# Attention backward on one core: three buffers for dV and dK, four for K^T and V^T, transposing DMAs placed tick by tick

## The chip, the cores and the metric

The kernel runs on one core of a Trainium2 chip. The metric is the device time of one execution in microseconds (us), lower is better; ten runs of the kernel before are at hand, and one of them was profiled.

## The reference

Two attention blocks, A and B, share the shapes: 8 batches, 96 query tokens, model width 640, 32 heads of 128, a cache of 512 keys. The outputs are the forward result and all gradients, so the keys and values are read and their gradients written for every head and batch.

```python
def block(x, k_cache, v_cache, wq, wo):       # x (8, 96, 640), caches (8, 32, 512, 128)
    q = (x @ wq).reshape(B, Sq, H, Dh).transpose(0, 2, 1, 3)
    scores = einsum("bhqd,bhkd->bhqk", q, k_cache) * (Dh ** -0.5)
    p = softmax(scores, axis=-1)
    o = einsum("bhqk,bhkd->bhqd", p, v_cache)
    return o.transpose(0, 2, 1, 3).reshape(B, Sq, H * Dh) @ wo

out, vjp = jax.vjp(f, A_x, A_k_cache, A_v_cache, A_wq, A_wo, B_x, ...)   # f joins A and B on the last axis
return (out, *vjp(grad_out))                  # out, dx, dk_cache, dv_cache, dwq, dwo of A and of B
```

All arrays are bf16.

## The kernel before, in words

The unit of work is one head of one batch. Two heads of one batch make a pair (HP = 2) and share their transfers: a pair needs K and V in natural layout (tiles K_sb and V_sb, L257), K^T and V^T by transposing DMA (KT_p and VT_p, L246), and it stores dV and dK (tiles dV_sb and dK_sb, L266). Each of these six transfers moves 256 KB and is issued on the queue of SP, which issues in order. There are 256 pairs in the two blocks.

An Emitter collects all steps with a tick and a slot and emits them sorted. In each tick one unit starts, and other units are in later stages of the same pipeline (offsets in OFF): S = QK^T and its row maximum (s2: PE L286, DVE L288, ACT's exponent L298), 1/rowsum and P (s3: DVE L308, POOL L317), P transposed and dV = P^T dO (s4: PE L340 and L357, ACT copies L346 and L362), O^T (s5: PE L333, DVE L343, POOL's product with dO L371), dP and dS (s6: PE L381 and L383, DVE L385), dS transposed and dK (s7: PE L407 and L423, ACT copies to dK_sb at L428), dQ^T (s8: PE L400). In between, at slots of their own, stand the steps of a whole head (projections, their transposes and the weight gradients; slot HEAD) and those of a group of four heads (output sums, gU; slot GRP). The last group of a block writes its sums through tile ob (DVE L521) and a DMA on POOL's queue (L522).

Block B's x and grad_out are brought in and transposed while block A is still running: ten chunks of 192 KB go through the staging tile ld_tmp (pool stp, DMA on POOL's queue L113, PE transposes L131).

The framework gives each tile a number of buffers, inserts the waits and orders the instructions by priority: an instruction that reuses a buffer waits until the last reader of its earlier content is done. PSUM is one set of eight banks that all steps share. A store's buffer is free when the store has landed. Each engine runs its instructions in the order of the built program.

Before, the four transposing DMAs of two batches (two K^T, two V^T) are emitted together, one tick ahead of the first one's s2; KT_p has four buffers, VT_p six, dV_sb and dK_sb two, ob five, ld_tmp three.

Of the kernel before, what the change touches and what calls it, by code (L numbers as in the profile page):

```python
# [11 lines left out]
BF16 = mybir.dt.bfloat16  # L12
# [3 lines left out]
class Emitter:  # L16
    def __init__(self):
        self.items = []
        self.n = 0
# [21 lines left out]
SL_GRP = 95  # L41
SL_SETUP = 96

OFF = dict(t=-1, kn=3, vn=0, s2=3, s3=3, s4=4, s5=5, s6=6, s7=7, s8=8)
HP = 2
TB = 2
HK = [
    dict(pA=-10, pB=-7, pC0=[-6, -4], pC1=[-5, -3], pD1=-2, pD0=0, qA0=21, qA1=25, qB=[28, 25], qD=[(26, 0, 2), (27, 2, 5)]),
    dict(pA=-4, pB=-2, pC0=[-1, 3], pC1=[1, 2], pD1=3, pD0=6, qA0=29, qA1=33, qB=[36, 33], qD=[(34, 0, 2), (35, 2, 5)]),
# [3 lines left out]
PRIO_OFF = 2000  # L53
GSPREAD1 = 9
SLOTS = dict(LOAD=0, S2A=5, S2B=5.5, S8=10, S7=20, S5=30, S4=40, S6=50, S3A=52, S3B=53, S5B=54, HEAD=SL_HEAD, GRP=SL_GRP)


def build_block(tc, em, tick0, blk, x, kc, vc, wq, wo, g_all, out_all, dx, dk, dv, dwq, dwo, ident, ones, pools, HG=4, first=True, groups=None):
    nc = tc.nc
# [7 lines left out]
    KC = Sk // 128  # L67
# [10 lines left out]
    while t0 < T:  # L78
        w = 512 if T - t0 >= 512 else (256 if T - t0 >= 256 else (128 if T - t0 >= 128 else T - t0))
# [4 lines left out]
    while c0 < D:  # L84
        w = 512 if D - c0 >= 512 else (256 if D - c0 >= 256 else 128)
# [10 lines left out]
    const, ps, kvp, wk, hd, hst, grp = (pools[k] for k in ("const", "ps", "kvp", "wk", "hd", "hst", "grp"))  # L96
# [7 lines left out]
    CS = pools["CS"]  # L104

    stp = pools["stp"]

    def setup_ld(which_, c):
        def f():
# [129 lines left out]
    F4 = Sk // R8 // KC  # L239

    def p_ldT(h, b, which):
        def f():
            key = "KT" if which == 0 else "VT"
            t_ = kvp.tile([128, F4 * KC, 16], BF16, name=key + "_p", bufs=(4 if which == 0 else 6))
            src = (kc if which == 0 else vc)[b, h:h + HP].rearrange("h (r f) d -> (h r) (f d)", r=R8)
            nc.sync.dma_start_transpose(t_[:], src)  # L246
            for j in range(HP):
                half = t_[:, :, j * R8:(j + 1) * R8]
                CS.setdefault((blk, h + j, b), {})[key] = half.rearrange("p (f c) r -> p f c r", c=KC)
        return f  # L250

    def p_ldn(h, b, which):
        def f():
            key = "K_sb" if which == 0 else "V_sb"
            t_ = kvp.tile([128, HP, KC, 128], BF16, name=key, bufs=4)
            src = (kc if which == 0 else vc)[b, h:h + HP]
            nc.sync.dma_start(t_[:].rearrange("p h c d -> p h (c d)"), src.rearrange("h (p c) d -> p h (c d)", c=KC))  # L257
            for j in range(HP):
                CS[(blk, h + j, b)][key] = t_[:, j]
        return f  # L260

    def p_st(h, b, which):
        def f():
            t_ = CS[(blk, h, b)]["dV_p" if which == 1 else "dK_p"]
            dst = (dv if which == 1 else dk)[b, h:h + HP]
            nc.sync.dma_start(dst.rearrange("h (p c) d -> p h (c d)", c=KC), t_[:])  # L266
            if which == 0:
                for j in range(HP):
                    CS.pop((blk, h + j, b))
        return f  # L270
# [79 lines left out]
    def c_s4(h, b):  # L350
        def f():
            st = CS[(blk, h, b)]
            hs = HS[(blk, h)]
            P_sb = st["P_sb"]
            dV_ps = bank([128, KC * 128], F32, "dV_ps")
            for c in range(KC):
                nc.tensor.matmul(dV_ps[:, c * 128:(c + 1) * 128], P_sb[:, c * 128:(c + 1) * 128], hs["dOnat_h"][:, b * 128:(b + 1) * 128], start=True, stop=True)  # L357
            j = h % HP
            if j == 0:
                st["dV_p"] = wk.tile([128, HP, KC * 128], BF16, name="dV_sb", bufs=2)  # L360
            dV_p = CS[(blk, h - j, b)]["dV_p"]
            nc.scalar.activation(dV_p[:, j], dV_ps[:], ACT.Identity, scale=1.0)  # L362
        return f
# [52 lines left out]
    def c_s7(h, b):  # L416
        def f():
            st = CS[(blk, h, b)]
            hs = HS[(blk, h)]
            dS_sb = st["dS_sb"]  # L420
            dK_ps = bank([128, KC * 128], F32, "dK_ps")
            for c in range(KC):
                nc.tensor.matmul(dK_ps[:, c * 128:(c + 1) * 128], dS_sb[:, c * 128:(c + 1) * 128], hs["Qnat_h"][:, b * 128:(b + 1) * 128], start=True, stop=True)  # L423
            j = h % HP
            if j == 0:
                st["dK_p"] = wk.tile([128, HP, KC * 128], BF16, name="dK_sb", bufs=2)
            dK_p = CS[(blk, h - j, b)]["dK_p"]
            nc.scalar.activation(dK_p[:, j], dK_ps[:], ACT.Identity, scale=1.0)  # L428
        return f
# [70 lines left out]
    def gU(g, which, t, gi):  # L500
        def f():
            acc = S.get("out_acc" if which == 0 else "dx_acc")
            dst_flat = out_flat if which == 0 else dx_flat
            (c0, w) = gsplits[gi]
            o_ps = bank([128, w], F32, "o_ps")
            for hh in range(groups[g]):
                h = GH0[g] + hh
                src = HS[(blk, h)]["OT_h"] if which == 0 else HS[(blk, h)]["dQT_h"]
                rhs = G[g]["wo_r"][:, hh, c0:c0 + w] if which == 0 else HS[(blk, h)]["wqT_h"][:, c0:c0 + w]
                nc.tensor.matmul(o_ps[:], src[:, t * 128:(t + 1) * 128], rhs, start=(hh == 0), stop=(hh == groups[g] - 1))  # L510
            if NG == 1:
                ob = wk.tile([128, w], BF16, name="ob", bufs=5)
                evac(EV["gU"], ob[:], o_ps[:])
                nc.gpsimd.dma_start(dst_flat[t * 128:(t + 1) * 128, c0:c0 + w], ob[:])
            elif g == 0:
                evac(EV["gU"], acc[:, t, c0:c0 + w], o_ps[:])
            elif g < NG - 1:
                nc.vector.tensor_tensor(acc[:, t, c0:c0 + w], o_ps[:], acc[:, t, c0:c0 + w], op=ALU.add)
            else:
                ob = wk.tile([128, w], BF16, name="ob", bufs=5)  # L520
                nc.vector.tensor_tensor(ob[:], o_ps[:], acc[:, t, c0:c0 + w], op=ALU.add)  # L521
                nc.gpsimd.dma_start(dst_flat[t * 128:(t + 1) * 128, c0:c0 + w], ob[:])  # L522
        return f
# [4 lines left out]
    for g in range(NG):  # L528
        h0 = GH0[g]
        for hh in range(groups[g]):  # L530
            h = h0 + hh
# [4 lines left out]
            em.add(c0t + hk["pB"], SL_HEAD, pB(h))  # L536
            em.add(c0t + OFF["s5"], SL_LOAD, h_alloc(h))
            for si in range(NTS):
# [4 lines left out]
            for b in range(B):  # L543
                ct = c0t + b * HP + j
                if j == 0:
                    if b % TB == 0:
                        for which in (0, 1):
                            for bb in range(b, b + TB):
                                em.add(ct + OFF["t"], SLOTS["LOAD"] - 1, p_ldT(h, bb, which))
                    em.add(ct + OFF["kn"], SLOTS["LOAD"], p_ldn(h, b, 0))  # L550
                    em.add(ct + OFF["vn"], SLOTS["LOAD"], p_ldn(h, b, 1))
                    em.add(ct + HP + OFF["s4"], SLOTS["LOAD"], p_st(h, b, 1))
                    em.add(ct + HP + OFF["s7"] + 1, SLOTS["LOAD"], p_st(h, b, 0))
                em.add(ct + OFF["s2"], SLOTS["S2A"], c_s2a(h, b))
                em.add(ct + OFF["s2"], SLOTS["S2B"], c_s2b(h, b))
                em.add(ct + OFF["s3"], SLOTS["S3A"], c_s3a(h, b))
                em.add(ct + OFF["s3"], SLOTS["S3B"], c_s3b(h, b))
                em.add(ct + OFF["s5"], SLOTS["S5B"], c_s5b(h, b))
                em.add(ct + OFF["s4"], SLOTS["S4"], c_s4(h, b))
                S45.setdefault(ct + OFF["s5"], [None, None, None])[0] = (blk, h, b)  # L560
                S45.setdefault(ct + OFF["s4"], [None, None, None])[1] = (blk, h, b)
                S45.setdefault(ct + OFF["s6"], [None, None, None])[2] = (blk, h, b)
                S78.setdefault(ct + OFF["s8"], [None, None])[0] = (blk, h, b)
                S78.setdefault(ct + OFF["s7"], [None, None])[1] = (blk, h, b)
                em.add(ct + OFF["s6"], SLOTS["S6"], c_s6(h, b))
                em.add(ct + OFF["s7"], SLOTS["S7"], c_s7(h, b))
# [24 lines left out]
def _kernel_impl(tc, A_x, A_k_cache, A_v_cache, A_wq, A_wo, B_x, B_k_cache, B_v_cache, B_wq, B_wo, grad_out,  # L591
           out_0, out_1, out_2, out_3, out_4, out_5, out_6, out_7, out_8, out_9, out_10, HG=4, slots=None, off=None, hk=None, ev=None, gspread=None, groupsA=None, groupsB=None):
    global GSPREAD0, GSPREAD1
    nc = tc.nc
# [10 lines left out]
    with ExitStack() as ctx:  # L605
        P = lambda **kw: ctx.enter_context(tc.tile_pool(**kw))
# [5 lines left out]
        pools = dict(  # L612
            const=P(name="const", bufs=1),
            ps=P(name="ps", bufs=8, space=PSUM),
            kvp=P(name="kv", bufs=11),
            wk=P(name="wk", bufs=3),
            hd=P(name="hd", bufs=2),
            hst=P(name="hst", bufs=8),
            grp=P(name="grp", bufs=1),
            stp=P(name="stp", bufs=3),  # L620
        )
        pools["S45"] = {}
        pools["S78"] = {}
        pools["HS"] = {}
        pools["CS"] = {}
        em = Emitter()
# [78 lines left out]
```

## Time and profile before

| | |
|---|---|
| median of 10 runs | 1761.67 us (1754.67 to 1767.12) |
| the profiled execution | 1765.31 us |
| its span (first to last instruction) | 1763.5 us |
| mean granted TensorE clock | 0.986 |
| HBM | 161.09 MB read, 159.12 MB written |
| PE / DVE / ACT / POOL busy | 1644.3 / 1391.8 / 1349.8 / 710.3 us |
| median issue to landing, stores of dV and dK | 4.0 and 4.1 us |
| median issue to landing, transposing DMAs | 5.0 to 5.3 us |

The profile is one execution. PE is TensorE's matmuls, PEld its weight loads, DVE the vector engine, ACT the scalar engine, POOL GpSimd, SP the engine that only issues DMAs. A number behind an L is a line of the kernel. "A <- B" after a wait names what ended it. A matmul's end is modelled, and a few matmul records can be missing.

### The profile page before, as it was taken

How to read it: one execution, taken by the hardware profiler on the slowest of the kernel's cores; microseconds unless marked ns; L12 is line 12 of the kernel's file. 1: busy time of each engine (PE TensorE's matmuls, PEld its weight loads, DVE VectorE, ACT ScalarE, POOL GpSimd, SP SyncE). 2: the span in 40 equal slices, each digit the busy share in tenths (PEclk: the TensorE clock that was granted, in tenths of full speed). 3: DMA queues.
4: the chain of work that ended last, by engine and by line, in shares of the span. 5: the costliest groups of instructions: out<-in, count | busy, mean ns of one | idle time of the engine just before them, and what ended most of it. 6: DMA issues, size and time to landing. Idle time of an engine off the chain costs nothing. (4 is left out here: it accounts for less than half of the span.)

```text
span 1763.5 us, 59487 instructions
## 1 busy us (share of the span) xinstructions
PE 1644.3 (93%) x22474; PEld 1370.9 (78%) x22648; DVE 1391.8 (79%) x3597; ACT 1349.8 (77%) x3529; POOL 710.3 (40%) x1306
## 2 busy tenths in 40 slices
PE   6899989999999999998998999999999999999997
PEld 5687878788787888777776787787878778787776
DVE  4786778878888888877776778887888878888886
ACT  4888967878778787866776888787787877778782
POOL 3333434433433443334365334333433334333346
PEclk9999999999999999999999999999999999999999
DMA  9999999999999999999899999999999999999993
GB/s 262 264 273 270 264 251 259 273 260 274 268 267 277 254 283 261 255 268 257 217 284 282 261 269 264 265 266 271 262 264 260 254 270 258 260 271 248 262 256 114
DMA packets 320609, 458.39 MB, mean 260 GB/s; under 512 B 37216, under 2 KB 300896, under 8 KB 312128
## 3 DMA queue, kind: packets, MB, share of 16 engines
q1 hardware_dynamic: 304672, 404.75, 88.1%
q0 software_dynamic: 15648, 49.83, 8.4%
q8 instruction: 177, 2.90, 0.7%
q14 instruction: 112, 0.92, 0.2%
HBM read 161.09 MB, written 159.12 MB: 182 GB/s over the span
## 5 line engine op out<-in xcount | busy, mean ns | idle before, releaser
L298 ACT ACTIVATE E_sb<-S_ps,negm 96x512 bf16<-96x512 f32 x512 | 349.3, 682 | 211.6 <-DVE negm L288 200.5
L317 POOL TENSOR_SCALAR P_sb<-E_sb,rinv 96x512 bf16<-96x512 bf16 x512 | 352.4, 688 | 344.0 <-DVE rinv L308 339.2
L371 POOL TENSOR_TENSOR prod<-OT_h,dOT_h 128x96 bf16<-128x96 bf16 x512 | 187.1, 365 | 570.1 <-DVE OT_h L343 566.2
L385 DVE SCALAR_TENSOR_TENSOR dS_sb<-dP_ps,dl_ps,P_sb 96x512 bf16<-96x512 f32 x512 | 381.9, 746 | 35.0 <-PE dl_ps L383 22.0
L288 DVE TENSOR_REDUCE negm<-S_ps 96x1 f32<-96x512 f32 x512 | 347.5, 679 | 71.1 <-PE S_ps L286 70.4
L428 ACT ACTIVATE dK_sb<-dK_ps 128x512 bf16<-128x512 f32 x512 | 302.9, 592 | 116.4 <-PE dK_ps L423 69.5
L362 ACT ACTIVATE dV_sb<-dV_ps 128x512 bf16<-128x512 f32 x512 | 307.8, 601 | 20.0 <-DMA out_dram<-dV_sb 17.4
L346 ACT ACTIVATE PT_sb<-optp_ps 128x384 bf16<-128x384 bf16 x512 | 252.3, 493 | 0.5 <-PE optp_ps L340 0.5
L286 PE MATMUL S_ps<-KT_p,QT_h 128*96 128x512 bf16 x512 | 196.4, 384 | 23.4 <-ACT dK_sb L428 22.7
L423 PE MATMUL dK_ps<-Qnat_h,dS_sb 96*128 96x128 bf16 x2048 | 199.8, 220 | 6.0 <-ACT dV_sb L362 4.7
L357 PE MATMUL dV_ps<-dOnat_h,P_sb 96*128 96x128 bf16 x2048 | 200.4, 221 | 3.6 <-ACT dV_sb L362 3.6
L407 PE MATMUL dq_dst_ps<-ident,dS_sb 96*128 96x96 bf16 x2048 | 174.1, 207 | 26.9 <-DVE dS_sb L385 24.8
L381 PE MATMUL dP_ps<-VT_p,dOT_h 128*96 128x512 bf16 x512 | 197.4, 386 | 0.3 <-ACT dV_sb L362 0.3
L409 DVE COPY dST_sb<-dq_dst_ps 128x384 bf16<-128x384 bf16 x512 | 176.9, 345 | 15.8 <-PE dq_dst_ps L407 15.1
L340 PE MATMUL optp_ps<-ident,P_sb 96*128 96x96 bf16 x2048 | 173.4, 206 | 2.7 <-POOL P_sb L317 1.8
L333 PE MATMUL optp_ps<-PT_sb,V_sb 128*128 128x96 bf16 x2048 | 173.4, 207 | 2.1 <-ACT PT_sb L346 1.9
L400 PE MATMUL dq_dst_ps<-dST_sb,K_sb 128*128 128x96 bf16 x2048 | 172.5, 207 | 3.0 <-ACT dK_sb L428 2.2
L510 PE MATMUL o_ps<-wo_r,OT_h 128*128 128x256 bf16 (+1 forms) x1152 | 153.6, 258 | 1.5 <-ACT E_sb L298 0.5
L400 PEld LDWEIGHTS <-K_sb 128*128 128x128 bf16 x2048 | 135.5, 99 | 24.3 <-issue 4.9
L510 PE MATMUL o_ps<-wqT_h,dQT_h 128*128 128x256 bf16 (+1 forms) x1152 | 150.3, 255 | 0.0
L343 DVE CAST OT_h<-optp_ps 128x96 bf16<-128x96 f32 x512 | 126.3, 247 | 29.7 <-PE optp_ps L340 26.8
L308 DVE RECIPROCAL rinv<-rowsum 96x1 f32<-96x1 f32 x512 | 79.9, 156 | 86.4 <-ACT E_sb L298 64.7
(77 smaller groups left out, 3397.5 us busy)
## 6 DMA issues: line engine op xcount, KB each, us to landing
out_dram<-dV_sb SPq DMA_DIRECT2D x256, 256.0 KB, 4.0
out_dram<-dK_sb SPq DMA_DIRECT2D x256, 256.0 KB, 4.1
V_sb<-in_A_v_cache_dram SPq DMA_DIRECT2D x128, 256.0 KB, 4.0
K_sb<-in_A_k_cache_dram SPq DMA_DIRECT2D x128, 256.0 KB, 4.4
V_sb<-in_B_v_cache_dram SPq DMA_DIRECT2D x128, 256.0 KB, 4.1
K_sb<-in_B_k_cache_dram SPq DMA_DIRECT2D x128, 256.0 KB, 4.9
out_dram<-dwo_sb POOLq DMA_DIRECT2D x64, 160.0 KB, 4.9
out_dram<-dwq_sb POOLq DMA_DIRECT2D x32, 320.0 KB, 6.3
```

Source lines behind the costliest of these rows:

```text
L288: nc.vector.tensor_reduce(negm[:], S_ps[:], axis=AX.X, op=ALU.max, negate=True)
L298: nc.scalar.activation(E_sb[:].rearrange("q (a f) -> q a f", f=F4), st["S_ps"][:].rearrange("q (f a) -> q a f", f=F4), ACT.Exp, bias=st["n ...
L317: nc.gpsimd.tensor_scalar(P_sb[:], st["E_sb"][:], st["rinv"][:], 0.0, op0=ALU.mult, op1=ALU.add)
L346: nc.scalar.activation(PT_sb[:], PT_ps, ACT.Identity, scale=1.0)
L357: nc.tensor.matmul(dV_ps[:, c * 128:(c + 1) * 128], P_sb[:, c * 128:(c + 1) * 128], hs["dOnat_h"][:, b * 128:(b + 1) * 128], start=True, s ...
L362: nc.scalar.activation(dV_p[:, j], dV_ps[:], ACT.Identity, scale=1.0)
L381: nc.tensor.matmul(dP_ps[:], hs["dOT_h"][:, tok], st["VT"], start=True, stop=True)
L385: nc.vector.scalar_tensor_tensor(dS_sb[:].rearrange("q (a f) -> q a f", f=F4), dP_ps[:].rearrange("q (f a) -> q a f", f=F4), dl_ps[:, 0:1] ...
L400: nc.tensor.matmul(dQT_ps, st["K_sb"][:, c, :], st["dST_sb"][:, c * Sq:(c + 1) * Sq], start=(c == 0), stop=(c == KC - 1))
L423: nc.tensor.matmul(dK_ps[:, c * 128:(c + 1) * 128], dS_sb[:, c * 128:(c + 1) * 128], hs["Qnat_h"][:, b * 128:(b + 1) * 128], start=True, s ...
L428: nc.scalar.activation(dK_p[:, j], dK_ps[:], ACT.Identity, scale=1.0)
L510: nc.tensor.matmul(o_ps[:], src[:, t * 128:(t + 1) * 128], rhs, start=(hh == 0), stop=(hh == groups[g] - 1))
```

## The change

The transposing DMAs are no longer emitted in groups of four: K^T of a pair is emitted two ticks ahead of the pair's start and V^T one tick behind it, each among the other loads. VT_p goes from six buffers to four, dV_sb and dK_sb from two to three; ob goes from five to four and ld_tmp from three to two. The ticks of the other loads and stores are the same numbers written as offsets, with slots that put loads of K^T and V^T ahead of plain loads ahead of stores within a tick. The object Chain passes SP's DMAs through and keeps the last one; it orders nothing.

```diff
-OFF = dict(t=-1, kn=3, vn=0, s2=3, ...)
+OFF = dict(kt=-2, vt=1, vn=0, kn=3, dv=6, dk=10, s2=3, ...)
-TB = 2
+class Chain:
+    def __call__(self, res):
+        ins = getattr(res, "ins", res)
+        self.last = ins
+        return res
...
-            t_ = kvp.tile([128, F4 * KC, 16], BF16, name=key + "_p", bufs=(4 if which == 0 else 6))
+            t_ = kvp.tile([128, F4 * KC, 16], BF16, name=key + "_p", bufs=4)
...
-            nc.sync.dma_start_transpose(t_[:], src)
+            sp(nc.sync.dma_start_transpose(t_[:], src))
...
-                st["dV_p"] = wk.tile([128, HP, KC * 128], BF16, name="dV_sb", bufs=2)
+                st["dV_p"] = wk.tile([128, HP, KC * 128], BF16, name="dV_sb", bufs=3)
...
-                st["dK_p"] = wk.tile([128, HP, KC * 128], BF16, name="dK_sb", bufs=2)
+                st["dK_p"] = wk.tile([128, HP, KC * 128], BF16, name="dK_sb", bufs=3)
...
-                ob = wk.tile([128, w], BF16, name="ob", bufs=5)
+                ob = wk.tile([128, w], BF16, name="ob", bufs=4)
...
-                    if b % TB == 0:
-                        for which in (0, 1):
-                            for bb in range(b, b + TB):
-                                em.add(ct + OFF["t"], SLOTS["LOAD"] - 1, p_ldT(h, bb, which))
-                    em.add(ct + OFF["kn"], SLOTS["LOAD"], p_ldn(h, b, 0))
-                    em.add(ct + OFF["vn"], SLOTS["LOAD"], p_ldn(h, b, 1))
-                    em.add(ct + HP + OFF["s4"], SLOTS["LOAD"], p_st(h, b, 1))
-                    em.add(ct + HP + OFF["s7"] + 1, SLOTS["LOAD"], p_st(h, b, 0))
+                    em.add(ct + OFF["kt"], SLOTS["LOAD"], p_ldT(h, b, 0))
+                    em.add(ct + OFF["vt"], SLOTS["LOAD"], p_ldT(h, b, 1))
+                    em.add(ct + OFF["vn"], SLOTS["LOAD"] + 0.1, p_ldn(h, b, 1))
+                    em.add(ct + OFF["kn"], SLOTS["LOAD"] + 0.1, p_ldn(h, b, 0))
+                    em.add(ct + OFF["dv"], SLOTS["LOAD"] + 0.2, p_st(h, b, 1))
+                    em.add(ct + OFF["dk"], SLOTS["LOAD"] + 0.2, p_st(h, b, 0))
...
-            stp=P(name="stp", bufs=3),
+            stp=P(name="stp", bufs=2),
+        pools["sp"] = Chain(tc)
```

More of the change, by code (lines that the diff above doesn't have):

```diff
@@ L42 @@
 SL_SETUP = 96
-OFF = dict(t=-1, kn=3, vn=0, s2=3, s3=3, s4=4, s5=5, s6=6, s7=7, s8=8)
+OFF = dict(kt=-2, vt=1, vn=0, kn=3, dv=6, dk=10, s2=3, s3=3, s4=4, s5=5, s6=6, s7=7, s8=8)
 HP = 2
-TB = 2
 HK = [
@@ L55, with __init__ @@
 SLOTS = dict(LOAD=0, S2A=5, S2B=5.5, S8=10, S7=20, S5=30, S4=40, S6=50, S3A=52, S3B=53, S5B=54, HEAD=SL_HEAD, GRP=SL_GRP)
+class Chain:
+    def __init__(self, tc):
+        self.tc = tc
+        self.last = None
+    def __call__(self, res):
+        ins = getattr(res, "ins", res)
+        self.last = ins
+        return res
 def build_block(tc, em, tick0, blk, x, kc, vc, wq, wo, g_all, out_all, dx, dk, dv, dwq, dwo, ident, ones, pools, HG=4, first=True, groups=None):
@@ L106, in build_block @@
     stp = pools["stp"]
+    sp = pools["sp"]
     def setup_ld(which_, c):
@@ L256, in f @@
             src = (kc if which == 0 else vc)[b, h:h + HP]
-            nc.sync.dma_start(t_[:].rearrange("p h c d -> p h (c d)"), src.rearrange("h (p c) d -> p h (c d)", c=KC))
+            sp(nc.sync.dma_start(t_[:].rearrange("p h c d -> p h (c d)"), src.rearrange("h (p c) d -> p h (c d)", c=KC)))
             for j in range(HP):
@@ L265, in f @@
             dst = (dv if which == 1 else dk)[b, h:h + HP]
-            nc.sync.dma_start(dst.rearrange("h (p c) d -> p h (c d)", c=KC), t_[:])
+            sp(nc.sync.dma_start(dst.rearrange("h (p c) d -> p h (c d)", c=KC), t_[:]))
             if which == 0:
@@ L519, in f @@
             else:
-                ob = wk.tile([128, w], BF16, name="ob", bufs=5)
+                ob = wk.tile([128, w], BF16, name="ob", bufs=4)
                 nc.vector.tensor_tensor(ob[:], o_ps[:], acc[:, t, c0:c0 + w], op=ALU.add)
```

## The prediction

> **What bounds the kernel now.** I read the page first (busy shares, then the DMA queues), then the windows of the steady part, then the waits of ACT and PE in it, and last the timeline around single stalls. Columns of the windows: stretch, its length, busy time and instructions of PE, weight loads, DVE, ACT and POOL, granted clock, DMA share, GB/s.
>
> ```profile
> PE 1644.3 (93%) x22474; PEld 1370.9 (78%) x22648; DVE 1391.8 (79%) x3597; ACT 1349.8 (77%) x3529; POOL 710.3 (40%) x1306
> ...
> q1 hardware_dynamic: 304672, 404.75, 88.1%
> ```
> ```profile
> 60.00:1700.00 1640.00, 1551.01 (x21309) 1294.42 (x21474) 1315.03 (x3409) 1286.63 (x3374) 653.23 (x1199) 0.99 0.99 264
> ```
>
> Two resources look full: PE (1551 of 1640 us in the steady part, 89 us without a matmul) and the DMA engines (0.99). Which one sets the pace is decided by what the others wait for. The waits of that stretch (total us, times, longest):
>
> ```profile
> ACT dK_sb L428 <- DMA out_dram<-dK_sb: 34.4, 30, 2.7
> ACT dV_sb L362 <- DMA out_dram<-dV_sb: 17.4, 16, 2.4
> ```
> ```profile
> PE S_ps L286 <- ACT dK_sb L428: 22.1, 14, 2.7
> PE dq_dst_ps L407 <- DVE dS_sb L385: 19.8, 17, 1.6
> PE dl_ps L383 <- POOL prod L371: 5.9, 1, 5.9
> PE tp_ps L131 <- DMA ld_tmp<-in_B_x_dram: 5.7, 3, 3.5
> PE dK_ps L423 <- ACT dV_sb L362: 4.7, 4, 1.6
> PE dV_ps L357 <- ACT dV_sb L362: 3.6, 6, 1.6
> PE nat_ps L441 <- ACT dK_sb L428: 2.8, 4, 1.2
> PE dq_dst_ps L400 <- ACT dK_sb L428: 2.2, 2, 1.2
> ```
>
> PE never waits for a load of K or V in any form. The DMAs that hold it are stores: ACT may not overwrite a dK_sb or dV_sb buffer whose store, two pairs ago, has not landed; its PSUM bank stays full, and PE, which needs the bank, stands. One such stall (start, length, then in brackets the idle time before and its releaser):
>
> ```profile
> 1317.92 0.19 ACT L298 ACTIVATION_READ_ACCUMULATOR E_sb<-S_ps,negm 96x1 f32 x1
> 1320.28 0.60 ACT L428 ACTIVATE dK_sb<-dK_ps 128x512 bf16<-128x512 f32 x1 [2.17 <-DMA out_dram<-dK_sb]
> ```
> ```profile
> 1320.93 0.38 PE L286 MATMUL S_ps<-KT_p,QT_h 128*96 128x512 bf16 x1 [2.16 <-ACT dK_sb L428]
> ```
>
> Is DMA the bound behind that? In 60 to 1700 us SP issues 1469 DMAs; their issue instructions sum to 1374 us, about 0.09 us lies between any two, and 143 us are spent waiting for PE or ACT to release a buffer. So per pair (six DMAs) SP needs 6 x (1374/1469 + 0.09) = 6.15 us; a pair lasts 1640/245 = 6.69 us. SP runs late by 2 to 6 us in places, but has spare time. From the landings in the trace, a K^T, V or K tile (four buffers each) lands 9.6 us or more before its first matmul, V^T (six buffers) mostly 29 us, whereas a dK or dV store lands only 2.4 us (median) before its buffer is rewritten, and at 0.1 us, that is, ACT was waiting, in over a tenth of the pairs. The stores are the one tight place.
>
> **The change, part by part.** Its time is summed against the profiled execution: 1765.3 us in all, span 1763.5. The runs have a median of 1761.7, so 3.6 us are taken off at the end.
>
> Third buffer for dK_sb and dV_sb. A store gets one more pair, 6.7 us, before its buffer is wanted; the longest ACT wait is 2.7 us. All these waits should go. On PE's path they are worth 22.1 + 4.7 + 3.6 + 2.8 + 2.2 and four smaller rows of the same two releasers (1.4, 1.3, 0.9, 0.3): 39.3 us. Bounds: 0, if a wait of another kind takes each place; 51.8, ACT's own sum. I take 39.3, PE's rows, and 6 us back, since some of those ticks have a next late thing (the dS_sb wait of 19.8 us in 17 places stays).
>
> The clock. After the longer of these stalls the granted clock is 0.50 for a while; five stretches follow stalls of this kind (at 240, 769, 889, 1216 and 1322 us), 20.5 us together. Here is the first and what comes after it:
>
> ```profile
> 240.10:246.90 6.80, 4.80 (x36) 3.65 (x36) 2.56 (x7) 3.87 (x10) 0.53 (x2) 0.50 1.01 265
> 246.90:260.00 13.10, 12.99 (x187) 11.11 (x188) 10.22 (x28) 8.53 (x23) 3.65 (x7) 1.00 1.01 242
> ```
>
> At half clock PE gets through half the work, so they cost up to 10.2 us. Bounds 0 to -10.2; I take all of it, as the stalls before them were only 1.9 to 2.7 us and would be gone. The Trainium skill (TensorE: Matmul & The Clock Gate, section "Part 1: The HAM clock gate") lets the clock drop only after an idle window of about 3.4 us. The trace here shows drops after shorter gaps; by the page's rule this term would be 0 and the sum 10.2 us weaker.
>
> V^T with four buffers instead of six. It loses two pairs of lead, 13.4 us. K^T has four already and its lead is the same seven ticks, with 9.7 us to spare at worst; V^T's worst in the steady part is 21 us, so about 8 stay. Cost 0; if the cover were gone, PE's dP matmul (L381) would wait, up to a landing of 5.2 us in a pair.
>
> Spreading the transposes, and the order. In the instruction order of the built programs PE's list is the same in both, DVE, ACT and POOL differ only around the change from block A to B and in the tail, and SP repeats the same six-DMA pattern: the scheduler of before had already pulled the groups of four apart as buffers came free. V^T followed directly by K^T stands 78 times in before and 79 in after. Each load waits for the same point of PE's order. Dependent loads, stores and what is queued behind them on SP keep their places: 0. The Chain object only records. At the start, K^T two ticks early and V^T two ticks later move two transposes behind the first V loads: within 1 us either way, taken as 0.
>
> Staging tile ld_tmp, two buffers instead of three. At the block change ten chunks of x and grad_out go through it; POOL issues the reload when PE has transposed the chunk in the buffer, and PE's transposes stand in PE's order, so a late chunk stops everything. The reloads land 5.5 us (median; 4.0 to 6.4) after issue, a tick takes 3.4 us.
>
> ```profile
> 831.51 0.87 POOL L113 DMA_DIRECT2D ld_tmp<-in_B_x_dram  x1 [0.17 <-issue]
> ...
> 833.92 0.69 POOL L317 TENSOR_SCALAR P_sb<-E_sb,rinv 96x512 bf16<-96x512 bf16 x1 [0.48 <-DVE rinv L308]
> ```
>
> That chunk reached PE at 837.9, a wait of 3.5 us; all four such waits of before sum to 6.3. With two buffers each chunk waits for the one two places ahead: 0.5 us of transposes and 5.5 of landing, 6.0 us for each two chunks instead of a tick of 3.4. Four such turns cost 4 x 2.6 = 10.4, less the 6.3 already paid: 4. Behind the waiting DMA on POOL stand P_sb (L317) and prod (L371), each needed a tick later, so they are covered unless the wait passes 3 us. One or two more half-clock stretches add 4. I take +8. Bounds: 0 (POOL's in-order queue already spaces them) and 38 (all eight reloads exposed, 8 x 5.5, less 6.3).
>
> ob with four buffers instead of five. DVE's wait for the store of ob is 12.2 us in 11 places now, most of it in the tail where POOL issues these stores 0.54 us apart. A fifth less depth adds some 3 us in the tail and 1 us at the end of block A: +4, bounds 0 and 12.2 (the wait doubles).
>
> Sum: -39.3 + 6 - 10.2 + 8 + 4 = -31.5. 1765.3 - 31.5 = 1733.8 for a profiled execution, less 3.6: 1730 us.
>
> **Rivals.** (1) Slower: SP is the bound after all. The queue runs late for 1252 of the 1469 DMAs, and stores with two buffers only show it first. Relieved of the stall, PE runs ahead until K^T or V^T is late, PE's stalls return on S_ps or dP_ps, and the costs of ld_tmp and ob remain: 1761.7 + 12 = 1774. It decides once six DMAs take SP 6.69 us instead of 6.15, for instance if V^T's issue (median 1.2 us) stretched by half a us towards K^T's 1.9 to 2.3. Against it: the 143 us in which SP waits for others, and the load margins, which stay above 9 us in the long stretches between stalls too. The Trainium skill (Perfetto Trace Analysis, section What "DMA-bound" means) reads an issuing sequencer that is solid DMA slices as a bound of its own; by that reading this rival is the forecast and the sum is +12. The waits for release speak against it here.
>
> (2) Half gain: the store waits go, but the ticks in which they stood are just as late from DVE (negm, dS_sb), so PE keeps half of the 39 us and the clock stretches: 1761.7 - 25 + 12 = 1749.
>
> (3) Full gain: all 49.5 us are won, and ld_tmp and ob are hidden: 1712.
>
> (4) The staging tile costs its upper bound of 38 instead of 8: -31.5 + 30 = -1.5, so 1760.
>
> The change not doing what it says is certain for the spread (the order shows it) and therefore in the forecast, not beside it.
>
> **How the numbers follow.** Forecast 0.64, (1) 0.10, (2) 0.13, (3) 0.08, (4) 0.05. A difference of 0.3%, about 5 us, is what a measurement of this kernel can tell from none. The forecast, (2) and (3) lie below 1756: faster 0.84 with a little of (2) moved to same; same 0.07 (most of (4), the tail of (2)); slower 0.09. The range goes from the full gain, 1711, up past the half gain to 1757, where (1) and (4) are left out.
>
> **What would show it.** Right: no wait of ACT L428 and L362 (L441 and L375 in the new numbering) for out_dram; PE at 0.96 to 0.97 in 60 to 1700; half-clock stretches only at the start, at the block change and near 945 us; waits of tp_ps for ld_tmp at 12 to 15 us; ob waits of 14 to 18 us. Wrong: PE waiting for DMA of KT_p or VT_p, SP's time for a pair at the tick's; or the same 39 us under another releaser; or a block change longer by 20 us or more.

## The result, and the profile after

The changed kernel has a median of 1745.8 us against 1764.9 us for the kernel before on the same chip: a ratio of 0.9899, with an interval of 0.9875 to 0.9923. That is 1.0% faster, 19 us by the medians, where the prediction had 32. The profiled execution after took 1748.35 us, its span is 1746.5 us, 17.0 us shorter than the span before, and its mean granted clock is 0.984.

First the page's busy times and its DMA queue, then the windows of the steady part (columns as in the prediction: stretch, length, PE, weight loads, DVE, ACT, POOL, granted clock, DMA share, GB/s):

```profile
PE 1641.7 (94%) x22474; PEld 1371.3 (79%) x22648; DVE 1390.6 (80%) x3597; ACT 1346.2 (77%) x3529; POOL 710.4 (41%) x1306
...
q1 hardware_dynamic: 304672, 404.75, 88.8%
```
```profile
60.00:1680.00 1620.00, 1547.03 (x21296) 1293.85 (x21459) 1312.87 (x3405) 1281.22 (x3365) 652.94 (x1198) 0.99 1.00 267
60.00:1700.00 1640.00, 1564.32 (x21554) 1307.86 (x21717) 1329.98 (x3448) 1299.12 (x3414) 661.83 (x1215) 0.99 1.00 266
```

From 60 to 1700 us PE is busy for 1564 us instead of 1551, 0.954 of the time where the prediction wanted 0.96 to 0.97. Now the waits of ACT and of PE in that stretch (total us, times, longest):

```profile
ACT dK_sb L441 <- DMA out_dram<-dK_sb: 19.6, 16, 3.0
...
ACT dV_sb L375 <- DMA out_dram<-dV_sb: 5.3, 5, 1.8
```
```profile
PE dq_dst_ps L420 <- DVE dS_sb L398: 21.3, 19, 1.5
PE S_ps L299 <- ACT dK_sb L441: 9.1, 6, 3.0
PE tp_ps L144 <- DMA ld_tmp<-in_B_x_dram: 7.6, 3, 4.0
PE nat_ps L454 <- ACT dK_sb L441: 6.6, 6, 2.2
...
PE dK_ps L436 <- ACT dV_sb L375: 2.4, 4, 1.2
PE tp_ps L144 <- DMA ld_tmp<-in_grad_out_dram: 1.8, 1, 1.8
PE dV_ps L370 <- ACT dV_sb L375: 1.6, 2, 0.9
```

ACT's waits for a store fell from 34.4 + 17.4 to 19.6 + 5.3 us, so half of them stayed although every store now has a pair more. On PE the rows of these two releasers, with three small ones of 0.9, 0.7 and 0.7 that are not shown, sum to 22.0 us instead of 39.3: 17.3 won. The chunks of x and grad_out cost 9.4 us instead of 6.3. PE still waits for no load of K or V.

Why do stores with three buffers still come late? SP's timeline says it (start, length of the issue instruction in us):

```profile
1103.13 1.17 SPq L259 DMA_TRANSPOSE VT_p<-in_B_v_cache_dram  x1
1104.39 2.87 SPq L259 DMA_TRANSPOSE KT_p<-in_B_k_cache_dram  x1
1107.36 0.53 SPq L279 DMA_DIRECT2D out_dram<-dV_sb  x1
1107.98 0.42 SPq L270 DMA_DIRECT2D V_sb<-in_B_v_cache_dram  x1
1108.49 0.45 SPq L279 DMA_DIRECT2D out_dram<-dK_sb  x1
1109.03 0.47 SPq L270 DMA_DIRECT2D K_sb<-in_B_k_cache_dram  x1
1109.60 1.14 SPq L259 DMA_TRANSPOSE VT_p<-in_B_v_cache_dram  x1
1110.83 2.64 SPq L259 DMA_TRANSPOSE KT_p<-in_B_k_cache_dram  x1
```

The queue is solid: about 0.1 us lies between two issues, and none of these waits for another engine. From 60 to 1700 us SP's issue instructions sum to 1473 us (before 1374), its waits for PE or ACT (a load waits until its buffer is free, a store until ACT has filled its tile) to 21 us (before 143), and 1467 of 1485 DMAs are issued late. A pair costs SP 6 x (1473/1485 + 0.09) = 6.49 us; the prediction had 6.15. What grew most is K^T's issue, which stands behind V^T's with at most one store between them: 2.22 us on average before, 2.49 after, while V^T's is 1.33 and 1.37. The third buffer gave PE more room, PE ran closer to SP, and SP, out of spare time, issued the stores later. From the end of ACT's copy to the issue of the store it takes 7.1 us for dK and 6.3 us for dV in the median, where it took 2.9 and 2.1 us before; issue to landing is about 4 us in both. So the median margin between a dK store's landing and its buffer's next use grew from 2.4 to 4.2 us, not by 6.7. The least margin of a K^T load fell from 9.7 to 4.2 us and that of V^T, which also lost two buffers, from 21 to 5.2 us.

### The profile page after: what moved, and what is told of

It reads as the page before. It is cut to its first block, busy times and chain, and to the rows that moved or that the text cites. A ratio compares the mean times of both kernels' runs of the same rounds, so it can differ in the third digit from the quotient of the medians.

```text
span 1746.5 us, 59484 instructions
## 1 busy us (share of the span) xinstructions
PE 1641.7 (94%) x22474; PEld 1371.3 (79%) x22648; DVE 1390.6 (80%) x3597; ACT 1346.2 (77%) x3529; POOL 710.4 (41%) x1306
```

## The experiments

Two theories were set against each other after the result. The queue theory (Q): SP has no spare time, because K^T's issue is stretched by V^T shortly ahead of it, so the order of the same DMAs on SP decides, and buffers only hide SP's lateness. The rival (D): the DMA engines themselves are full, with a share of 0.99, so that only less data or more buffers help. A separate question was what each part of the change is worth. SP's sums below are of 60 to 1700 us, issue instructions first and waits for PE or ACT second. Each ratio is against the kernel before on the same chip, whose median was 1758.7 to 1765.4 us by chip; kernels that ran on different chips are compared by their ratios.

**The buffers of dV, dK and V^T alone**, in the kernel before (transposes in groups of four, ob and ld_tmp as they were):

```diff
-            t_ = kvp.tile([128, F4 * KC, 16], BF16, ..., bufs=(4 if which == 0 else 6))
+            t_ = kvp.tile([128, F4 * KC, 16], BF16, ..., bufs=4)
-                 st["dV_p"] = wk.tile(..., name="dV_sb", bufs=2)     # the same for dK_sb
+                 st["dV_p"] = wk.tile(..., name="dV_sb", bufs=3)
```

> The kernel before with three buffers for dV_sb and dK_sb and four for VT_p; transposing DMAs still in groups of four, ob five, ld_tmp three. Theory A (the gain is the store buffers', and the trimmed ob and ld_tmp cost about 7 us of it): 1765 - 26 = 1739 us, ratio 0.985, with PE's waits for ACT's dK_sb and dV_sb near 22 us instead of 39. Theory B (the trimmed tiles cost nothing): ratio 0.990 as the changed kernel. Theory C (the new ticks of the transposes bring part of the gain): ratio above 0.993.

Measured: 1727.6 us, ratio 0.981 (0.9776 to 0.9844). ACT's waits for stores are 14.4 and 4.6 us, SP 1457 and 35.5. This part alone is better than the whole change, and PE waits for no V^T load in it, so the loss of two buffers shows nowhere. Even here store waits remain.

**The new ticks alone**: the changed kernel with two buffers of dV and dK, five of ob and three of ld_tmp; V^T keeps its four. (Before, a group of four transposes was emitted one tick ahead of its first pair's start, which is four ticks ahead of that pair's s2.)

```diff
-                 st["dV_p"] = wk.tile(..., name="dV_sb", bufs=3)     # the same for dK_sb
+                 st["dV_p"] = wk.tile(..., name="dV_sb", bufs=2)
-                 ob = wk.tile([128, w], BF16, name="ob", bufs=4)     # in both places
+                 ob = wk.tile([128, w], BF16, name="ob", bufs=5)
-             stp=P(name="stp", bufs=2),
+             stp=P(name="stp", bufs=3),
```

> The changed kernel with dV_sb and dK_sb back at two buffers, ob at five and ld_tmp at three, so only the new ticks and V^T's four buffers are left of the change. Theories A and B: ratio 1.000 within 0.003, store waits as before (ACT 50 us). Theory C: 0.995 or less. A loss of V^T's lead would show as waits of dP_ps for VT_p and a ratio over 1.003.

Measured: 1784.1 us, ratio 1.0125 (1.0079 to 1.0171). ACT's wait, which is 34.4 us in 30 places before, grew:

```profile
ACT dK_sb L441 <- DMA out_dram<-dK_sb: 44.4, 34, 2.6
```

SP's sums are those of before (1368 and 151), so it has no more work. The new ticks cost 1.25% when the stores have no slack.

**The smaller staging alone**: the kernel before with four ob and two ld_tmp buffers.

```diff
-                 ob = wk.tile([128, w], BF16, name="ob", bufs=5)     # in both places
+                 ob = wk.tile([128, w], BF16, name="ob", bufs=4)
-             stp=P(name="stp", bufs=3),
+             stp=P(name="stp", bufs=2),
```

> The kernel before with ob at four buffers and ld_tmp at two, nothing else. Theory A: 1765 + 7 = 1772 us, ratio 1.004, the block change longer by about 6 us (waits of tp_ps 9 us and more half clock) and 1 us in the tail. Theory B: 1.000.

Measured: 1766.1 us, ratio 1.0033 (1.001 to 1.0056), or 5.8 us. The waits for chunks of x doubled from 5.7:

```profile
PE tp_ps L131 <- DMA ld_tmp<-in_B_x_dram: 11.6, 4, 4.4
```

From the first to the last chunk transposed it takes 29.9 us instead of 26.8, and the tail from the last S_ps to the end 43.1 instead of 40.8.

**The change without the smaller staging**: the changed kernel with five ob and three ld_tmp buffers (the last two edits of the new ticks' diff).

> The changed kernel with ob back at five and ld_tmp back at three buffers. Theory A: 0.985, like the three-buffer kernel with grouped transposes. Theory B: 0.990, as the changed kernel. Theory C: as the changed kernel or better, and at least 0.003 below the kernel with grouped transposes.

Measured: 1738.8 us, ratio 0.9872 (0.9834 to 0.991). ACT still waits 28.9 us for dK's store, twice the 14.4 of the first experiment with the same buffers; SP 1472 and 18.6. What separates the two kernels is only the ticks and slots, that is, SP's order: in the two traces the instructions of PE, DVE, ACT and POOL come in the same order.

**Stores ahead of loads.** In the order of the programs one thing sets them apart: in the kernel before, the dK store goes ahead of the V load of the same tick in 59 of 250 pairs; after, never, since the stores' slot comes behind the loads'. One such place in the profile before:

```profile
1108.73 0.53 SPq L266 DMA_DIRECT2D out_dram<-dV_sb  x1
1109.35 0.42 SPq L266 DMA_DIRECT2D out_dram<-dK_sb  x1
1109.87 0.46 SPq L257 DMA_DIRECT2D V_sb<-in_B_v_cache_dram  x1
```

So, on top of the last kernel:

```diff
-                    em.add(ct + OFF["dv"], SLOTS["LOAD"] + 0.2, p_st(h, b, 1))
-                    em.add(ct + OFF["dk"], SLOTS["LOAD"] + 0.2, p_st(h, b, 0))
+                    em.add(ct + OFF["dv"], SLOTS["LOAD"] - 0.2, p_st(h, b, 1))
+                    em.add(ct + OFF["dk"], SLOTS["LOAD"] - 0.2, p_st(h, b, 0))
```

> The changed kernel with ob five and ld_tmp three buffers (as the run before with 0.987) and one more edit: the stores' slot is 0.2 ahead of the loads instead of 0.2 behind them, so that in about 60 of 256 pairs SP issues the dK store ahead of the V load again. Theory S (the loss of the new ticks is the stores' place behind the loads): 0.981, and ACT's wait for the dK store near 14 us instead of 29. Rival T (the ticks of the transposes themselves cost it): stays at 0.987.

Measured: 1733.7 us, ratio 0.9822 (0.9792 to 0.9851). The dK store is ahead of the V load in 59 pairs again; its wait fell from 28.9 to 19.6 us, dV's to 1.3. The direction fits, and the ratio is that of the first experiment (0.981), but the intervals of this and the last kernel overlap, so I repeated it where the stores have no slack, on the kernel of the new ticks alone:

> The kernel with the new ticks alone (1.0125: dV_sb and dK_sb two buffers, V^T four, ob five, ld_tmp three) with the stores' slot ahead of the loads'. Theory S (with two buffers the loss was the stores' place behind the loads): 1.000 within 0.004, ACT's wait for the dK store near 34 us again. Rival T (the transposes' ticks or V^T's four buffers): 1.010 or more.

Measured: 1765.2 us, ratio 1.0017 (0.9986 to 1.0048), where the same kernel with stores behind loads had 1.0125 (1.0079 to 1.0171). The intervals are apart. The wait for dK's store fell by a third, that for dV's rose from 16.4 to 21.8:

```profile
ACT dK_sb L441 <- DMA out_dram<-dK_sb: 29.4, 25, 2.1
...
ACT dV_sb L375 <- DMA out_dram<-dV_sb: 21.8, 18, 3.0
```

So the loss through the new ticks was the place of the stores behind the loads, and nothing else of the ticks, nor V^T's four buffers, shows in the time.

**The transposes really apart.** The scheduler of both kernels puts K^T directly behind V^T in 78 and 79 pairs and mostly one dV store between them in the rest. Here SP's order is written out, with no wait added: each of SP's DMAs is given an order-only dependence on the one before it. The order is K^T, V load, dK store, V^T, K load, dV store; buffers as in the fourth experiment. Two things differ from there: the two transposes are apart, and each store stands one pair earlier among the loads.

```diff
-OFF = dict(kt=-2, vt=1, vn=0, kn=3, dv=6, dk=10, s2=3, ...)
+OFF = dict(kt=-2, vt=0, vn=0, kn=3, dv=5, dk=8, s2=3, ...)
...
+        if self.last is not None:
+            self.tc.add_manual_dep(ins, self.last.name, mybir.DependencyInfo(
+                mybir.DependencyClass.NoSync, mybir.DependencyReason.DATA), reason="sp order")
...
-                    em.add(ct + OFF["vt"], SLOTS["LOAD"], p_ldT(h, b, 1))
+                    em.add(ct + OFF["vt"], 61, p_ldT(h, b, 1))
-                    em.add(ct + OFF["dv"], SLOTS["LOAD"] + 0.2, p_st(h, b, 1))   # the same for dk
+                    em.add(ct + OFF["dv"], 60, p_st(h, b, 1))
```

> Same buffers; SP's order is written out as K^T, V, dK store, V^T, K, dV store for every pair, so that two plain DMAs stand between any two transposing ones; all other engines' orders are unchanged. Theory Q (SP's issue time is the bound, and a K^T right behind V^T is what stretches it): mean issue of K^T from 2.5 to below 1.9 us, SP's waits for release above 100 us instead of 19, 0.975. Theory D (the DMA engines are the bound and issue only shows their back-pressure): SP's total issue time stays near 1470 us, time as without it, 0.985 to 0.99. V^T issued later: its margin falls by up to 3 us, no wait expected.

Measured: 1703.8 us, ratio 0.9652 (0.9627 to 0.9676). K^T's issue is 1.58 us on average, SP's sums 1349 and 139, ACT's store waits 0.9 us. PE waits once, 1.0 us, for a K^T load.

**The same with the dK store ahead of the V load** (the V load's slot becomes 60.5): K^T, dK store, V load, V^T, K load, dV store.

> As the run with the transposes apart, with the dK store ahead of the V load in every pair: K^T, dK store, V, V^T, K, dV store. Theory S: ACT's wait for the dK store below 10 us and 0.003 to 0.005 faster than with V first. If a dK store that is not yet ready holds the queue instead: V and V^T late, SP's waits for release grow by 50 us or more, time not better than with V first.

Measured: 1702.5 us, ratio 0.9638 (0.9614 to 0.9662), the fastest kernel of this study, though its interval overlaps that of the one above, and the 0.003 to 0.005 expected from the earlier dK store did not show. The instruction orders of PE, DVE, ACT and POOL are those of the fourth experiment, so the 0.0234 between the two ratios come from SP's order alone. SP's timeline, to be read against that of the changed kernel above:

```profile
1103.89 0.42 SPq L272 DMA_DIRECT2D V_sb<-in_B_v_cache_dram  x1
1104.41 1.15 SPq L261 DMA_TRANSPOSE VT_p<-in_B_v_cache_dram  x1
1105.61 1.20 SPq L272 DMA_DIRECT2D K_sb<-in_B_k_cache_dram  x1
1107.74 0.38 SPq L281 DMA_DIRECT2D out_dram<-dV_sb  x1
1108.22 1.13 SPq L261 DMA_TRANSPOSE KT_p<-in_B_k_cache_dram  x1
1111.10 0.38 SPq L281 DMA_DIRECT2D out_dram<-dK_sb  x1
```

K^T's issue takes 1.13 us instead of 2.6 to 2.9, and there are gaps again (1106.8 to 1107.7, 1109.4 to 1111.1) in which SP waits until ACT has filled the store's tile. The sums are 1229 and 270 us, and nearly all of the 270 us stand ahead of stores: a store is now issued 0.05 us (median) or less after ACT's copy ends, not 6 to 7 us. The windows, and PE's waits in 60 to 1700 us:

```profile
60.00:1680.00 1620.00, 1570.51 (x21874) 1316.06 (x22041) 1345.33 (x3495) 1309.97 (x3447) 673.76 (x1238) 1.00 1.00 273
```
```profile
PE dq_dst_ps L419 <- DVE dS_sb L397: 23.4, 23, 1.4
PE dl_ps L395 <- POOL prod L383: 7.3, 1, 7.3
PE tp_ps L146 <- DMA ld_tmp<-in_B_x_dram: 3.5, 3, 1.6
```

No wait for a store of dK or dV and none for a load of K or V is left. The DMA share is 1.00 as in the changed kernel, but the GB/s are 273 instead of 267: a full share was no bound. PE is at 0.97 of this stretch, and its waits are for DVE, POOL and, with 3.5 us, the chunks of x.

**Less data, the same order** (the test of D): the fourth experiment's kernel, but each store writes 256 of the 512 elements of a row, so half of dK and dV is left out.

```diff
-            sp(nc.sync.dma_start(dst.rearrange("h (p c) d -> p h (c d)", c=KC), t_[:]))
+            sp(nc.sync.dma_start(dst.rearrange("h (p c) d -> p h (c d)", c=KC)[:, :, 0:256], t_[:, :, 0:256]))
```

> The changed kernel with ob five and ld_tmp three buffers, where each store of dV and dK writes only half of each row (256 of 512 elements for each partition and head), so part of the two gradients is left out; number and order of the DMAs are the same, packets have 512 instead of 1024 bytes. Theory D: some 0.6 us less DMA work for each pair, K^T's issue shortens, SP waits for release 100 us or more, time 0.97. Theory Q: issue time unchanged near 1470 us, time 0.985 (only the stores' own landing is shorter, which takes away part of ACT's waits).

Measured: 1704.4 us, ratio 0.9656 (0.963 to 0.9683); no store waits, SP 1313 and 176. K^T's issue, still behind V^T, fell to 1.98 us on average. So an issue's length is no fixed price: it also depends on how much the DMA engines have to do, and the time comes down by either remedy to the same 1702 to 1704 us. Neither theory holds alone in its strict form. D falls in that the same bytes in another order reach the same time; Q in that fewer bytes relieve SP without any reordering.

**Is the third buffer needed then?** The order of the fastest kernel with two buffers of dV and dK and six of V^T, as in the kernel before.

> The buffers of the kernel before (dV_sb and dK_sb two, VT_p six, ob five, ld_tmp three) with SP's order written out as in the 0.964 run: K^T, dK store, V, V^T, K, dV store. If the queue's lateness alone made the store waits: 0.965 to 0.97, ACT's store waits below 10 us with two buffers. If the third buffer is needed too: ACT waits 20 us or more, 0.975 to 0.99.

Measured: 1703.8 us, ratio 0.9691 (0.9673 to 0.9709). The store wait is nearly gone without the third buffer:

```profile
ACT dK_sb L440 <- DMA out_dram<-dK_sb: 3.6, 5, 1.4
```

Whether the third buffer is worth anything on top is not settled: by the ratios (0.9691 and 0.9638, intervals apart) it is 0.5%, by the medians, taken on two chips, 1.4 us.

**The smaller staging under the good order**: the fastest kernel with four ob and two ld_tmp buffers, that is, the changed kernel's own buffers.

> The changed kernel's own buffers (ob four, ld_tmp two) with that written order, so that SP's order is the only difference from the changed kernel: 1765 x 0.964 + 7 = 1709 us, 0.968, if the trimmed tiles cost the same here as in the kernel before (+0.0033); up to 0.972 if they cost more where nothing else holds PE; 0.964 if nothing.

Measured: 1710.2 us, ratio 0.9721 (0.9704 to 0.9739). From the first to the last chunk it takes 25.9 us against 21.8 in the fastest kernel, and the tail 43.2 against 41.5: 5.8 us together. That is most of the 7.7 us between the medians, but these two kernels ran on different chips, and by the ratios 0.0083, some 15 us, lie between them; the rest is not accounted for.

**Written out, but adjacent** (the control): the same order-only dependences and buffers as the fastest kernel, with V^T moved to just ahead of K^T (`vt=-1`): K^T, dK store, V load, K load, dV store, V^T.

> As the 0.964 run, with V^T moved directly ahead of K^T in every pair (K^T, dK store, V, K, dV store, V^T): order written out too, same buffers. If the distance between the transposing DMAs is what counts: K^T's mean issue 2.4 us or more, SP's waits for release below 50 us, 0.98 to 0.99. If the written order or the early dK store did it: 0.965 to 0.97.

Measured: 1723.1 us, ratio 0.979 (0.9758 to 0.9821), 0.0152 above the fastest, and 0.0099 above the written order with two store buffers, which ran on the same chip. K^T's mean issue is 2.38 us. K^T's issues in block B of five kernels (count: least/median/longest in ns, first and last start): before, the change, the fastest, the adjacent and the one with half stores.

```profile
L246 SPq DMA_TRANSPOSE KT_p<-in_B_k_cache_dram x128: 1096/2312/9590, 851.7 to 1705.5; - x128
```
```profile
L259 SPq DMA_TRANSPOSE KT_p<-in_B_k_cache_dram x128: 1102/2452/5524, 851.9 to 1688.7; - x128
```
```profile
L261 SPq DMA_TRANSPOSE KT_p<-in_B_k_cache_dram x128: 1095/1194/4554, 823.5 to 1646.1; - x128
```
```profile
L261 SPq DMA_TRANSPOSE KT_p<-in_B_k_cache_dram x128: 1209/2215/4666, 834.9 to 1670.9; - x128
```
```profile
L259 SPq DMA_TRANSPOSE KT_p<-in_B_k_cache_dram x128: 1095/1912/8020, 818.5 to 1642.9; - x128
```

The least is 1.1 to 1.2 us everywhere; the median follows what stands ahead, and with half the store bytes it is lower though V^T stands as close. Adjacent, SP is full again (1491 and 23). ACT waits for no store, but this time loads are late at PE, 13.0 us in all:

```profile
PE optp_ps L345 <- DMA V_sb<-in_B_v_cache_dram: 5.7, 5, 1.7
...
PE S_ps L298 <- DMA KT_p<-in_B_k_cache_dram: 3.0, 4, 1.7
```

So it is the distance between the two transposing DMAs that makes most of the difference, not that the order is written out: 0.0152 of the 0.0234. The other 0.0082, from the fourth experiment to this kernel, go with the rest of the written order, such as the stores' earlier place; the runs do not split them further.

Could K^T's issue be short in the fastest kernel only because SP pauses there? In 108 of its 247 pairs from 60 to 1700 us SP does not pause (0.2 us or more) between V^T and K^T, and the median issue there is 1.32 us, against 1.14 us in the others; in the kernel with the V load ahead of the dK store, 158 such pairs have 1.54 us. So the pauses shorten it a little, but without them it is still well below the 2.17 us of the adjacent order. Whether the two plain DMAs count or the time that they take can't be told from these runs.

## Why the prediction was right, and where it was wrong

The direction, and the place in the trace where the time came from, were right; the gain was 19 us and not 32. On the prediction's own base (1761.7 us) the ratio gives 1744 us, nearer to rival (2)'s 1749 than to the forecast's 1730; but only that rival's size fits, not its reason, since PE's wait for dS_sb is 21.3 us instead of 19.8 and the half that stayed is still waits for stores. Of the five signs named for being right, only the last, the waits for ob, came as stated. The runs split the gain. The buffers alone are worth 0.019 of 1764.9, or 33.5 us; the ticks and slots take back 0.0062 (from 0.981 to 0.9872, intervals that just overlap), about 11 us; the smaller staging takes back 0.0027 (0.9872 to 0.9899, not apart by their intervals), about 5 us, or 5.8 us measured alone.

- **The third buffer, "-39.3 + 6", with the clock's "-10.2".** Together -43.5 in the prediction, -33.5 by the first experiment. In the profile of the change itself, where the ticks work against it, the term is -17.3. The failed step is "All these waits should go": it took a store's lateness as fixed at 2.7 us and gave it 6.7 us more, but SP's lateness grew as soon as PE ran closer to it: a dK store is issued 7.1 us after its data are ready instead of 2.9, which eats 4.2 of the 6.7 us.
- **The clock.** Three stretches after store stalls remained, 17.1 us instead of 20.5, so 1.7 us at half clock were won and not 10.2. The first, with ACT's and PE's records of the stall and the windows of it and what follows:

```profile
233.10 0.60 ACT L441 ACTIVATE dK_sb<-dK_ps 128x512 bf16<-128x512 f32 x1 [2.96 <-DMA out_dram<-dK_sb]
```
```profile
233.75 0.59 PE L299 MATMUL S_ps<-KT_p,QT_h 128*96 128x512 bf16 x1 [2.96 <-ACT dK_sb L441]
```
```profile
233.00:239.80 6.80, 6.05 (x49) 4.89 (x49) 3.59 (x10) 3.87 (x10) 1.05 (x2) 0.50 0.92 273
239.80:253.00 13.20, 13.09 (x184) 11.09 (x185) 9.91 (x28) 9.32 (x24) 3.12 (x7) 1.00 0.99 260
```

  A gap of 2.96 us, and from its last 0.8 us on 6.8 us at 0.50; the other two come with gaps of 2.66 and 2.18 us. The measurement decides against a strict reading of the Trainium skill's rule (TensorE: Matmul & The Clock Gate, section "Part 1: The HAM clock gate") that the clock drops only after an idle window of about 3.4 us. The mechanism of the term was right; it failed in size, because the stalls stayed.
- **ld_tmp and ob, "+8" and "+4".** Right in direction, about double in size: 5.8 us alone. In the profile after, the stretch from first to last chunk grew by 5.0 us, of which 3.1 are waits of tp_ps (9.4 us in all, where the sign was 12 to 15) and much of the rest half clock (13.65 us there instead of 6.83), and the tail by 2.1 us. One chunk's wait of 4.04 us, again with half clock behind it:

```profile
820.99 0.29 PE L144 MATMUL tp_ps<-ident,ld_tmp 128*128 128x128 bf16 x1 [4.04 <-DMA ld_tmp<-in_B_x_dram]
```
```profile
DVE ob L534 <- DMA out_dram<-ob: 17.9, 20, 4.6
```

  The waits for ob, 12.2 us before, came out at 17.9, as "14 to 18" had it.
- **V^T's four buffers, "0".** Right as far as the runs go: PE never waits for V^T in the first experiment nor after the change, though its least margin came out at 5.2 us and not at about 8.
- **"Spreading the transposes, and the order: ... 0".** This step failed. That SP's pattern of six stayed, with V^T directly ahead of K^T as often as before, was right. But "stores ... keep their places" was not: the dK store lost its place ahead of the V load in 59 of 250 pairs. With no slack for stores that cost 1.25%, and giving the place back took the loss to 0.17%, which can't be told from nothing.
- **"SP runs late ..., but has spare time".** This is the reading on which the forecast was preferred to rival (1), and it was too kind. The 143 us of waiting for release were real, but the price of an issue is not fixed: it rose from 6.15 to 6.49 us per pair, close to the 6.69 that the rival named as its point, in the way it named (the stretch of an issue between V^T and K^T, though on K^T's side). No load came late, so the rival's end did not come (it came in the adjacent kernel, where PE waits 13.0 us for loads); its mechanism ate the missing part. The Trainium skill (Perfetto Trace Analysis, section What "DMA-bound" means) reads a sequencer solid with DMA slices as a bound, and the slices as descriptor generation. The runs agree in part: relieving SP by order alone, with the buffers of the kernel before, took 3.1% off. They differ on what fills it: the same DMAs, no larger and no fewer, took 1229 us of issue instead of 1473.

The rows of the profile do not close: -17.3 - 1.7 + 5.0 + 2.1 = -11.9 us against a span shorter by 17.0. The other 5 us lie in smaller gaps and other stretches of half clock that I did not assign. Also open is what inside the DMA path stretches K^T's issue behind V^T; the runs show that distance and less store data both shorten it, not why. And it is open how much of the 0.0082 is due to the stores' place.

## What to carry to other kernels

When a store buffer is late, look first at the queue that issues the stores: sum its issue instructions and its waits for release, and distrust spare time in it if one kind of issue is far longer in the median than at its least (here 2.3 us against 1.1). Reorder that queue before adding buffers, with two plain DMAs between any two transposing ones, and a store ahead of loads that are not urgent; here the order alone brought 3.1% with the old buffers, the third buffers alone 1.9%. Emitting DMAs at other ticks is not yet an order: read where the scheduler put them.

## What the hardware showed that I had not expected

A transposing DMA's issue on SP takes 1.1 us at its least. K^T's median from 60 to 1700 us is 2.2 to 2.6 us directly behind V^T, 1.8 us (before) and 2.4 us (after) with one store between, and 1.1 to 1.3 us with two plain DMAs between, SP's pauses included. Half the store bytes, with no reordering, took its median over all pairs from 2.4 to 1.9 us. The busy share of the DMA engines was 0.98 to 1.03 in every kernel with whole stores, while the GB/s went from 263 to 273, so that share did not tell how much room there was; with half stores it was 0.93, at 231 GB/s.

There is no single length of gap that brings half clock. In the steady part of the profiles before and after, every PE gap of 2.66 us or more came with a stretch of it. Of the shorter ones a gap of 1.58 us (at 84 us, before) and one of 2.18 us (at 1418 us, after) came with one, while one of 2.27 us (at 1107 us, before) did not. These stretches lasted 3.41 or 6.83 us, and 10.24 us once in the changed kernel and once in the fastest, with waits of 6.1 and 7.3 us for prod.
